# Batch 1's frequency-domain products: three instead of four

## The chip, the cores and the metric

The kernel runs on one core of one Trainium2 chip. The time is the device time of one execution, in microseconds (us). The kernel before takes 871.36 us, the median of three runs (871.35 to 871.52).

The engines have short names in the profile: PE is TensorE (PEld its weight loads), DVE is VectorE, ACT is ScalarE, POOL is GpSimd, and SP is SyncE, which only issues DMAs here. Each engine works through its own queue in order.

## The reference

```python
def _attn_ref(x, w_r, w_i, b_r, b_i):          # x: 8 x 3008 x 256
    X = np.fft.rfft(x, axis=1)
    Xr, Xi = (X.real.astype(np.float32), X.imag.astype(np.float32))
    Yr = Xr @ w_r - Xi @ w_i + b_r
    Yi = Xr @ w_i + Xi @ w_r + b_i
    lam = 0.01
    Yr = np.sign(Yr) * np.maximum(np.abs(Yr) - lam, 0.0)
    Yi = np.sign(Yi) * np.maximum(np.abs(Yi) - lam, 0.0)
    Y = Yr.astype(np.float64) + 1j * Yi.astype(np.float64)
    return np.fft.irfft(Y, n=x.shape[1], axis=1).astype(np.float32)

def _moe_ref(x, w_in, w_out):                  # x: 24064 x 256, d_ff 2048
    h = x @ w_in
    g = np.where(h > 0.0, h, np.exp(np.minimum(h, 0.0)) - 1.0)
    return (g @ w_out).astype(np.float32)
```

The output of the first is the input of the second: a Fourier transform along the sequence, a complex 256 x 256 layer with soft shrinkage (subtract from each value its clip to plus or minus 0.01), the transform back, and a feed-forward layer with an elu between two matrices.

## The kernel before

**Stages of one batch.** The transforms of length 3008 = 47 x 64 are split in two factors and done by matmuls. A batch passes through A (six units: the first factor), a round trip through DRAM that turns the data into the tile `Z`, X (eight units, `unit_X`: the second factor, giving `XT`, real and imaginary parts with features on the partitions), M (twelve groups of 128 frequencies, `unit_M`, numbered q = 0 to 5, i = 0 or 1: the complex layer and the shrinkage, giving the tile `Y`), DMAs that turn `Y` into `Yx` (`turn_Y`), B (six units, the first factor back; B v reads `Yx` of q = v), another round trip through DRAM (`Bs`), and Y (eight units, "y" or "n" in the plan, giving `yT`, the input of the feed-forward layer). `unit_X` for batch 1 takes its units in the order of quarters: units 2g and 2g + 1 give the slots 8g to 8g + 7 of the 32 slots for the two halves of the features.

**The loop.** The feed-forward layer is cut into 376 steps, 47 for a batch. Step i has a `front` (four products into the two PSUM tiles `hps`, one per 128 hidden units, then ScalarE's exponentials into `Et`), an elu (`elu` clips `Et`, `finish_elu` makes `gT` from `hps` and `Et` on VectorE at L1159 or L1161, one step later), and a `back` two steps later (eight products of `gT` with `w_out_r` into `ps_o`). There are four `hps` tiles, so the front of step i + 2 needs the two that the elu of step i has read. While the feed-forward layer of batch b runs, `plan(b)` hangs the stages of batch b + 1 and the A units of b + 2 into its steps, as lists `f0` (before the front) and `f1` (after `finish_elu`). Batch 1 has its stages in the steps of batch 0: X in steps 10 to 17 (`lead` = `FILL` = 10), M groups 0,0 to 2,1 in steps 18 to 23, B0 in 24, M 3 in 25 and 26, B1 in 27, M 4 in 28 and 29, B2 in 30, M 5 in 31 and 32, B3 to B5 in 33 to 35, and A of batch 2 from 36 on. In every eighth step (17, 25, 33) VectorE copies half of a finished output block (L1203).

**Where the elu's clip runs.** In a step with an M group ScalarE does it with a second pass (`on_act`: L1128 and L1133). In a "pooled" step GpSimd clips `Et` (L1169, two instructions). Else VectorE does it (L1171, one instruction of 128x1024). In the steps of batch 0 from 10 on, steps with other work are not pooled.

**M of batches 2 to 7.** With s = Xr + Xi the two outputs need three products of 256 columns, each over the two halves of the features: k = s @ w_r, and the products of Xi and Xr with changed weights (w_i plus or minus w_r, made in place by `three_weights`, L276, which also changes the bias, L279). `unit_M` puts k into one PSUM bank (`k1`) and the other two into another (`ps`). VectorE adds bias and k (L340), then k to both others (L341); GpSimd adds the second bias (L346), clips (L349) and subtracts (L350). The sums s are made by GpSimd beforehand (`sum_XT`, L260, rows of 512 frequencies); the last of six rows lies in the tile `busy`. `three_weights` runs in the first four steps of batch 1's feed-forward layer (47 to 50).

**M of batches 0 and 1.** They use the plain weights: four products of 512 columns into one bank (`m_group`, L292), one VectorE addition of the bias (L302), and for batch 1 GpSimd's clip and subtraction (L314, L315). `turn_Y` issues four DMAs for each q on SP's queue (L429); for batch 1's last q, two of the four go on GpSimd's.

GpSimd's queue carries also the loads of `x` for the batch after next (`load_x`, L121, steps 12, 15 and 18 here) and, in step 12, a small copy (`gate`, L976) that waits until batch 1's `Z` has arrived.

Of the kernel before, what the change touches and what calls it, by code (L numbers as in the profile page):

```python
# [8 lines left out]
ALU = mybir.AluOpType  # L9
# [15 lines left out]
NS = 32  # L25
# [4 lines left out]
def kernel(  # L30
# [224 lines left out]
    def sum_XT(b, dt, chunks=range(3)):  # L255

        XT = XT_of[b]
        for ch in chunks:
# [2 lines left out]
                sum_of(dt, ch), XT[:, dt, 0, m], XT[:, dt, 1, m], ALU.add  # L261
            )

    def sum_of(dt, ch):

        if 3 * dt + ch == 5:
            return busy[:]
        if not XS_of:
            XS_of.append(sump.tile([P, 5, 512], BF16, name="XS", tag="XS"))
        return XS_of[0][:, 3 * dt + ch]  # L270

    def three_weights(c, dt):
# [4 lines left out]
        if c == dt == 0:  # L277
            b_r_, b_i_ = (bias_bc[:, D * k : D * k + D] for k in range(2))
            nc.gpsimd.tensor_tensor(b_i_, b_i_, b_r_, ALU.subtract)  # L279

    mps_of = {}

    def m_group(b, q, i, ps, biased=False):
        XT = XT_of[b]
# [22 lines left out]
        return yb, clip  # L307

    def unit_M(b, q, i):
        if b == 1:  # L310
            if i == 0:
                mps_of[q] = unit_ps("mps", False)
            yb, clip = m_group(b, q, i, mps_of[q][:, i, :])
            nc.gpsimd.tensor_scalar(clip[:], yb, LAM, -LAM, ALU.min, ALU.max)  # L314
            nc.gpsimd.tensor_tensor(Y_of[b, q][:, i, :], yb, clip[:], ALU.subtract)  # L315
            return
        XT, o = XT_of[b], (2 * q + i) * P
        if i == 0:
            Y_of[b, q] = wk4.tile([P, 2, 2 * D], BF16, name="Y", tag="Y")
        ps, k1 = (  # L320
            last_banks("psM").tile([P, 2 * D], F32, name="mps", tag="mps") for _ in range(2)
        )
        ch, oc = divmod(o, 512)
        r, s = wcat_r, wcat_s
        todo = [
            (k1[:, 0:D], None, r[:, :, 0:D]),
            (ps[:, 0:D], XT[:, :, 1, o : o + P], s[:, :, 0:D]),
            (ps[:, D : 2 * D], XT[:, :, 0, o : o + P], s[:, :, D : 2 * D]),
        ]
        if o == 0 and b > 3:  # L330
            todo.append(todo.pop(0))
        for out_, lhs, w in todo:
            for dt in range(2):
                nc.tensor.matmul(  # L334
                    out_, lhsT=lhs[:, dt] if lhs is not None else sum_of(dt, ch)[:, oc : oc + P],
                    rhs=w[:, dt, :], start=(dt == 0), stop=(dt == 1),
                )
        yb = wk3.tile([P, 2 * D], F32, name="yb", tag="yb")
        clip = wk2.tile([P, 2 * D], F32, name="clip", tag="clip")
        nc.vector.tensor_tensor(yb[:, D : 2 * D], k1[:, 0:D], bias_bc[:, 0:D], ALU.add)  # L340
        nc.vector.tensor_tensor(  # L341
            yb[:].rearrange("p (c d) -> p c d", c=2),
            ps[:].rearrange("p (c d) -> p c d", c=2),
            yb[:, D : 2 * D].unsqueeze(1).to_broadcast([P, 2, D]), ALU.add,
        )
        nc.gpsimd.tensor_tensor(  # L346
            yb[:, D : 2 * D], yb[:, D : 2 * D], bias_bc[:, D : 2 * D], ALU.add
        )
        nc.gpsimd.tensor_scalar(clip[:], yb[:], LAM, -LAM, ALU.min, ALU.max)  # L349
        nc.gpsimd.tensor_tensor(Y_of[b, q][:, i, :], yb[:], clip[:], ALU.subtract)  # L350

    held = []

# [868 lines left out]
    def plan(b):  # L1222

        f0 = [[] for _ in range(PER)]
        f1 = [[] for _ in range(PER)]
        mode = [None] * PER
        n1, n2 = b + 1, b + 2
        mid = [("X", u) for u in range(8)] + [
# [4 lines left out]
        ]  # L1233
        if n1 < B:
            if b:
                lead, xs = 0, (3, 6, 9)

                def M(q):
                    return [("M", q, 0), ("M", q, 1)]

                shift = b - 1 if b < 3 else b - 3
                seq = [("y", 2), ("y", 3)] + [None] * shift + [("X", u) for u in range(8)]
                if b < 3:
                    seq += [("y", 4)] + M(0) + M(1) + [("y", 5)] + M(2) + [("B", 0)]
                else:
                    seq += M(0) + [("y", 4)] + M(1) + [("y", 5)] + M(2) + [("B", 0)]
                seq += [("y", 6), ("B", 1)] + M(3) + [("y", 7), ("B", 2)]
                on_act = [("X", 4), ("X", 7)]
                if b < 3:
                    seq += M(4) + [("B", 3)] + M(5) + [("A", 0), ("B", 4), ("A", 1), ("A", 2)]  # L1250
                    seq += [("B", 5), ("A", 3), ("A", 4), ("A", 5), None]
                else:
                    seq += M(4) + [("B", 3), ("A", 0)] + M(5) + [("B", 4)]
                    seq += [("A", 1), ("A", 2), ("A", 3), ("B", 5), ("A", 4), ("A", 5)] + [None] * (3 if n2 == B else 2)
                seq += [("n", 0), ("n", 1)]
            else:
                lead, seq = FILL, mid
                xs = (12, 15, 18)
        else:
            lead, seq = 0, [("y", u) for u in range(2, 8)]  # L1260
        for t, u in enumerate(seq, lead):
            if u is None:
                continue
            if b and n1 < B:
                mode[t] = "act" if u in on_act or u[0] == "M" else "pool"
            if mode[t] == "act" and u[0] != "M":
                k = {"y": "Y"}.get(u[0], u[0])
                c = {"y": b, "A": n2}.get(u[0], n1)
                if c < B:
                    dve = (False, True) if k == "B" else (k != "X" or b < 3 and u[1] == 7,)  # L1270
                    f0[t].append(put(k, c, u[1], False, *dve))
            elif u[0] == "y":
                f0[t].append(put("Y", b, u[1]))
            elif u[0] == "n":
                f0[t].append(put("Y", n1, u[1]))
            elif u[0] == "A":
                if n2 < B:
                    f0[t].append(put("A", n2, u[1]))
            elif b == 0 and u == ("B", 5):
                f0[t].append(put("B", n1, 5, False, True))  # L1280
            else:
                f0[t].append(put(u[0], n1, *u[1:]))
            if u[0] == "M" and u[2] == 1:
                f1[t].append((turn_Y, (n1, u[1])))
            if u == ("B", 5):
                for w, k in enumerate((0, 2, 3, 4)):
                    f1[t + k].append((load_Bs, (n1, w, 0, 4 * K1 - 16 * (b == w == 0))))
            if u == ("A", 5) and n2 < B:
                for part in ((0, 8), (8, NS)):
                    f1[t] += [(load_Z, (n2, a, *part)) for a in range(3)]  # L1290
        if b == 0:
            for t in range(6):
                f1[t].append((unit_A, (1, t, False, t not in (0, 2), True)))
            for t, a, u in (
                (7, f0, 2), (7, f1, 3), (8, f0, 4), (8, f1, 5), (9, f0, 6), (9, f1, 7)
            ):
                a[t].append((split_Y, (0, u)))
            for w in range(1, 4):
                f1[w].append((load_Bs, (0, w)))
            f1[6].append((turn_M3, ()))  # L1300
            for part in ((0, 8), (8, NS)):
                f1[5] += [(load_Z, (1, a, *part)) for a in range(3)]
            f1[xs[0]].append((lambda: gate(Z[:, 16, 0:1]), ()))
        if n2 < B:
            for ci in range(3):
                f1[xs[ci]].append((load_x, (n2, ci)))
        if b and n1 < B:
            f0[seq.index(("X", 4))].append((sum_XT, (n1, 0)))
            f0[seq.index(("X", 7))].append((sum_XT, (n1, 1, range(2 if b < 3 else 3))))
            if b < 3:  # L1310
                f0[seq.index(("M", 2, 0))].insert(0, (sum_XT, (n1, 1, (2,))))
        return f0, f1, mode
# [4 lines left out]
    for i in range(n + LAG):  # L1317
# [6 lines left out]
        elif i < n:  # L1324
# [9 lines left out]
            if mode[r]:  # L1334
                on_act = mode[r] == "act"
                pooled = not on_act
            else:
                on_act = any(f is unit_M for f, a in f0[r])
                pooled = free or i < FILL
            third = calm and bare % 3 == (2 if i // PER == B - 1 else 1)  # L1340
            h = front(i, third, on_act)
        finish_elu()
        if i < n:
# [50 lines left out]
```

## Time and profile before

| What | us |
|---|---|
| median of three runs | 871.36 |
| profiled execution | 871.1 |
| its span | 869.3 |
| TensorE busy | 860.8 |
| ScalarE busy | 715.4 |
| VectorE busy | 666.2 |
| GpSimd busy | 592.8 |

The span runs from the first to the last instruction that the profiler recorded; the execution's own time holds a little more. Busy shares are means over stages with different limits, so the stages around the change are read one by one. The chain of work that ended last is followed back from the last instruction through what released each piece; 94% of it is TensorE. In rows of the timeline the start of a TensorE group lies up to 0.35 us ahead of the start that the chain gives, since matmuls overlap; the two are not mixed where a difference is formed.

### The profile page before, as it was taken

What the parts mean: (1) busy time and instruction counts of PE and PEld (TensorE: products, weight loads), DVE (VectorE), ACT (ScalarE), POOL (GpSimd) and SP (SyncE); (2) the same over time, 40 slices, a digit from 0 to 9 for tenths busy, and PEclk for the clock granted to TensorE, in tenths of its full rate; (3) what the DMA queues carried; (4) which work ended last, traced back from release to release, by engine and by line L of the source; (5) the groups of instructions that cost most, each with busy time, mean ns of one, the idle gap of its engine ahead of it and who ended that gap; (6) DMA issues with size and microseconds to landing.
All of it is one profiled execution on the core that took longest, in us unless ns stands there. A gap on an engine that the chain in (4) does not pass through costs nothing.

```text
span 869.3 us, 18553 instructions
## 1 busy us (share of the span) xinstructions
PE 860.8 (99%) x6773; PEld 675.8 (78%) x6773; DVE 666.2 (77%) x1103; ACT 715.4 (82%) x1255; POOL 592.8 (68%) x866
## 2 busy tenths in 40 slices
PE   8999999999999999999999999999999999999997
PEld 6567677887788877887778877787877888787776
DVE  8889779697676886778866787677777687788775
ACT  8878888888978889798887988879887888876664
POOL 8671651898657986588846987459874697734664
PEclk9999999999999999999999999999999999999999
DMA  8897446532575135653365432753337313250111
GB/s 248 282 288 213 117 131 193 164 117 73 141 224 170 51 79 168 191 170 92 89 183 172 128 104 78 217 165 107 94 96 213 90 39 85 79 141 25 40 36 49
DMA packets 113597, 116.11 MB, mean 134 GB/s; under 512 B 11569, under 2 KB 103473, under 8 KB 110145
## 3 DMA queue, kind: packets, MB, share of 16 engines
q1 hardware_dynamic: 108512, 86.74, 35.2%
q0 software_dynamic: 4704, 27.92, 9.8%
q8 instruction: 53, 0.87, 0.4%
q14 instruction: 40, 0.32, 0.1%
q10 hardware_dynamic: 288, 0.26, 0.1%
HBM read 53.28 MB, written 48.23 MB: 117 GB/s over the span
## 4 chain that ended last, share of the span: by engine, by line
PE 94%; POOL 2%; DVE 1%; DMA 1%; ACT 1%; issue 0%; DVEq 0%; POOLq 0%
PE ps_o L1192 39%; PE hps L1118 34%; PE mps L334 5%; PE xps L242 3%; PE mps L1118 2%; PE yps L615 2%; PE bps L451 2%; PE mps L292 2%; PE aps L194 2%; POOL Y L350 1%; DMA xt<-in_x_dram 1%; PE aps L186 0%; POOL yb L346 0%; POOL clip L349 0%; DVE gT L1159 0%
## 5 line engine op out<-in xcount | busy, mean ns | idle before, releaser
L1159 DVE SCALAR_TENSOR_TENSOR gT<-Et,hps 128x512 fp32r<-128x512 f32 x630 | 403.1, 682 | 137.0 <-POOL Et L1169 127.0
L1192 PE MATMUL ps_o<-w_out_r,gT 128*128 128x256 f32 x3008 | 477.2, 301 | 0.0
L1192 PEld LDWEIGHTS ps_o<-w_out_r,gT 128*128 128x128 f32 x3008 | 404.4, 189 | 48.0 <-DVE osb L1203 0.2
L1169 POOL TENSOR_SCALAR Et<-Et 128x512 f32<-128x512 f32 x482 | 287.3, 615 | 203.1 <-ACT Et L1130 201.6
L1118 PE MATMUL hps<-yT,w_in_s 128*128 128x512 bf16 (+7 forms) x1620 | 366.7, 353 | 0.3
L1130 ACT ACTIVATE Et<-hps 128x512 f32<-128x512 f32 x514 | 282.7, 610 | 41.7 <-PE hps L1118 38.6
L1118 PEld LDWEIGHTS <-w_in_s 128*128 128x128 bf16 x1728 | 144.1, 98 | 104.7 <-issue 13.1
L1128 ACT ACTIVATE Et<-hps 128x512 f32<-128x512 f32 x192 | 104.5, 597 | 42.0 <-PE hps L1118 41.6
L1133 ACT ACTIVATE Et<-Et 128x512 f32<-128x512 f32 x192 | 110.5, 632 | 0.0
L350 POOL TENSOR_TENSOR Y<-yb,clip 128x512 bf16<-128x512 f32 x72 | 92.7, 1287 | 6.0
L346 POOL TENSOR_TENSOR yb<-yb,bias_bc 128x256 f32<-128x256 f32 x72 | 53.2, 738 | 11.3 <-DVE yb L341 11.2
L150 ACT CAST XT<-xps 128x768 bf16<-128x768 f32 x57 | 45.8, 804 | 14.1 <-PE xps L242 13.9
L341 DVE TENSOR_TENSOR yb<-mps,yb 128x512 f32<-128x512 f32 x72 | 49.8, 692 | 7.2
L150 ACT CAST yT<-yps 128x752 bf16<-128x752 f32 x56 | 44.1, 787 | 13.7 <-PE yps L615 13.5
L1161 DVE SCALAR_TENSOR_TENSOR gT<-hps,Et 128x512 fp32r<-128x512 f32 x78 | 50.2, 686 | 3.3
L349 POOL TENSOR_SCALAR clip<-yb 128x512 f32<-128x512 f32 x72 | 44.1, 613 | 6.3
L150 ACT CAST A<-aps 128x1024 bf16<-128x1024 f32 x40 | 40.7, 1018 | 8.1 <-PE aps L194 5.0
L150 ACT CAST Bz<-bps 128x1024 bf16<-128x1024 f32 x41 | 41.6, 1014 | 5.3 <-PE bps L451 5.0
L340 DVE TENSOR_TENSOR yb<-mps,bias_bc 128x256 f32<-128x256 f32 x72 | 30.5, 424 | 17.5 <-PE mps L334 15.7
L334 PE MATMUL mps<-wcat_s,XT 128*128 128x256 bf16 x288 | 43.2, 273 | 0.0
L1203 DVE COPY osb<-ps_o 128x512 f32<-128x512 f32 x46 | 31.7, 690 | 5.4 <-PE ps_o L1192 3.4
L260 POOL TENSOR_TENSOR XS<-XT 128x512 bf16<-128x512 bf16 x30 | 34.1, 1157 | 2.4 <-ACT XT L150 1.4
(216 smaller groups left out, 673.3 us busy)
## 6 DMA issues: line engine op xcount, KB each, us to landing
xt<-in_x_dram POOLq DMA_DIRECT2D x21, 1024.0 KB, 5.3
out_dram<-osb SPq DMA_DIRECT2D x154, 128.0 KB
Bs<-DB SPq DMA_DIRECT2D x30, 384.0 KB
Yx<-Y SPq DMA_DIRECT2D x166, 64.0 KB
DA<-A SPq DMA_DIRECT2D x19, 512.0 KB
DB<-Bz SPq DMA_DIRECT2D x19, 512.0 KB
Z<-DA SPq DMA_DIRECT2D x21, 384.0 KB
xt<-in_x_dram POOLq DMA_DIRECT2D x6, 512.0 KB, 6.2
```

Of the source, the lines that this page charges most:

```text
L150: nc.scalar.copy(dst, src)
L334: nc.tensor.matmul(out_, lhsT=lhs[:, dt] if lhs is not None else sum_of(dt, ch)[:, oc : oc + P], rhs=w[:, dt, :], start=(dt == 0), stop=(d ...
L346: nc.gpsimd.tensor_tensor(yb[:, D : 2 * D], yb[:, D : 2 * D], bias_bc[:, D : 2 * D], ALU.add)
L350: nc.gpsimd.tensor_tensor(Y_of[b, q][:, i, :], yb[:], clip[:], ALU.subtract)
L1118: nc.tensor.matmul(hps[s][:, c0:c1], lhsT=w_in_s[:, dt, ft * P : ft * P + P], rhs=yT_of[b][:, dt, t0 : t0 + c1 - c0], start=(dt == 0), sto ...
L1128: nc.scalar.activation(Et[:, s], hps[s], AF.Relu, scale=-1.0)
L1130: nc.scalar.activation(Et[:, s], hps[s], AF.Exp)
L1133: nc.scalar.activation(Et[:, s], Et[:, s], AF.Exp, scale=-1.0)
L1159: nc.vector.scalar_tensor_tensor(o, e, -1.0, h, ALU.add, ALU.max)
L1161: nc.vector.scalar_tensor_tensor(o, h, 0.0, e, ALU.max, ALU.add)
L1169: nc.gpsimd.tensor_scalar(e, e, 1.0, 0.0, ALU.min, ALU.max)
L1192: nc.tensor.matmul(po[q][:, j, :], lhsT=gT[:, s, i_ * P : i_ * P + P], rhs=w_out_r[:, ft, :], start=(ft == 0 and j == 0), stop=(ft == NFT ...
```

## The change

Batch 1's M groups take the form of the other batches: `unit_M` loses its branch for batch 1 (the old `m_group` stays for batch 0). What goes with it:

- `sum_part(b, g)`, new, makes the sums for one quarter of `Z`'s slots, in steps 11, 13, 15 and 17. Its three instructions go over runs of eight neighbouring elements, 48, 32 and 16 of them, 32 elements from one run to the next.
- The first group's product with the sums comes last of its three (as already for batches 4 and later).
- `three_weights` runs in steps 10 to 13 instead of 47 to 50.
- In the steps of B0, B1 and B2 of batch 1 the elu's clip is pooled.
- In batch 1's last group (q = 5, i = 1) VectorE clips and subtracts the real half at once; GpSimd clips the imaginary half, and VectorE subtracts it in `finish_Y`, after the elu of the step before and ahead of `turn_Y`'s DMAs. These DMAs stand in the order they had: for each half of the partitions one of the real half on SP's queue and one of the imaginary half on GpSimd's.

```diff
+    def sum_part(b, g):
+        XT, k = XT_of[b], slice(8 * g, 8 * g + 8)
+        def by_m(v):
+            return v.rearrange("p (m s) -> p m s", s=NS)[:, :, k]
+        sum_of(0, 0)
+        XS, m = XS_of[0][:], 2 * 512
+        for out_, dt, m0, m1 in (
+            (XS[:, 0:3].rearrange("p c n -> p (c n)"), 0, 0, 3 * 512),
+            (XS[:, 3:5].rearrange("p c n -> p (c n)"), 1, 0, m),
+            (busy[:], 1, m, 3 * 512),
+        ):
+            nc.gpsimd.tensor_tensor(
+                by_m(out_), by_m(XT[:, dt, 0, m0:m1]), by_m(XT[:, dt, 1, m0:m1]), ALU.add
+            )
...
     def unit_M(b, q, i):
-        if b == 1:
-            if i == 0:
-                mps_of[q] = unit_ps("mps", False)
-            yb, clip = m_group(b, q, i, mps_of[q][:, i, :])
-            nc.gpsimd.tensor_scalar(clip[:], yb, LAM, -LAM, ALU.min, ALU.max)
-            nc.gpsimd.tensor_tensor(Y_of[b, q][:, i, :], yb, clip[:], ALU.subtract)
-            return
...
-        if o == 0 and b > 3:
+        if o == 0 and (b == 1 or b > 3):
             todo.append(todo.pop(0))
...
+        if (b, q, i) == (1, 5, 1):
+            Y, h = Y_of[b, q][:, i, :], slice(0, D)
+            nc.vector.tensor_scalar(clip[:, h], yb[:, h], LAM, -LAM, ALU.min, ALU.max)
+            nc.vector.tensor_tensor(Y[:, h], yb[:, h], clip[:, h], ALU.subtract)
+            h = slice(D, 2 * D)
+            nc.gpsimd.tensor_scalar(clip[:, h], yb[:, h], LAM, -LAM, ALU.min, ALU.max)
+            late_Y.append((Y[:, h], yb[:, h], clip[:, h]))
+            return
...
+    def finish_Y():
+        Y, yb, clip = late_Y.pop()
+        nc.vector.tensor_tensor(Y, yb, clip, ALU.subtract)
...
             if u[0] == "M" and u[2] == 1:
+                if (b, u[1]) == (0, 5):
+                    f1[t].append((finish_Y, ()))
                 f1[t].append((turn_Y, (n1, u[1])))
...
-        if b and n1 < B:
+        if b == 0:
+            for g in range(4):
+                f0[lead + 2 * g + 1].append((sum_part, (n1, g)))
+        elif n1 < B:
...
-                pooled = free or i < FILL
+                pooled = free or i < FILL or any(f is unit_B and a[1] < 3 for f, a in f0[r])
...
-            if PER <= i < PER + 4:
-                three_weights(*divmod(i - PER, 2))
+            if FILL <= i < FILL + 4:
+                three_weights(*divmod(i - FILL, 2))
```

More of the change, by code (lines that the diff above doesn't have):

```diff
@@ L279, in three_weights @@
             nc.gpsimd.tensor_tensor(b_i_, b_i_, b_r_, ALU.subtract)
-    mps_of = {}
     def m_group(b, q, i, ps, biased=False):
@@ L348, in unit_M @@
         )
+        if (b, q, i) == (1, 5, 1):
[6 more added lines that the diff above has]
+            return
         nc.gpsimd.tensor_scalar(clip[:], yb[:], LAM, -LAM, ALU.min, ALU.max)
         nc.gpsimd.tensor_tensor(Y_of[b, q][:, i, :], yb[:], clip[:], ALU.subtract)
+    late_Y = []
+    def finish_Y():
+        Y, yb, clip = late_Y.pop()
+        nc.vector.tensor_tensor(Y, yb, clip, ALU.subtract)
     held = []
```

## The prediction

> **What bounds the kernel now.** I read the page's engine totals first, then the chain of work that ended last around batch 1's M groups, then the timelines of VectorE (DVE) and GpSimd (POOL) there and in batch 2, which already works in the new form. Totals, and busy time by stretch (stretch and its length, then PE, PEld, DVE, ACT, POOL):
>
> ```profile
> PE 860.8 (99%) x6773; PEld 675.8 (78%) x6773; DVE 666.2 (77%) x1103; ACT 715.4 (82%) x1255; POOL 592.8 (68%) x866
> 66.46:83.78 17.32, 17.32 (x161) 13.95 (x162) 15.51 (x25) 14.73 (x25) 1.58 (x3) 1.00 0.86 234
> 83.78:99.82 16.04, 16.04 (x99) 10.73 (x97) 12.22 (x21) 12.54 (x25) 10.82 (x13) 1.00 0.47 133
> ```
>
> TensorE is busy all the time at the full granted clock, in the eight X steps (66.46 to 83.78) and in the six M groups (83.78 to 99.82) alike; POOL is nearly idle in the X steps, and VectorE has 1.8 us spare in 17.3. So TensorE's work is the time, as long as nobody keeps it waiting. The chain (start, length, piece), first batch 1's M groups, then batch 2's:
>
> ```profile
> 83.78 0.88 PE mps L292 x4
> ...
> 99.82 0.45 PE bps L451 x4
> ...
> 105.65 0.86 PE hps L1118 x4
> ...
> 127.19 0.45 PE bps L451 x4
> ...
> 129.46 0.46 PE aps L194 x2
> ...
> 197.51 0.59 POOL Et L1169
> 198.10 0.02 issue
> 198.12 0.70 DVE gT L1159
> 198.82 0.04 issue
> 198.87 0.59 PE hps L1118 x2
> 199.46 0.59 PE hps L1118 x2
> ...
> 200.97 0.67 PE mps L334 x6
> ...
> 203.45 0.67 PE mps L334 x6
> ```
>
> Before, TensorE goes through batch 1's six groups without a gap. In batch 2 it does not: a POOL clip that came late (197.51) held an elu on VectorE, and that held TensorE, whose four hps products took 1.19 instead of 0.86 us.
>
> **The matmuls.** A group now takes 0.88 us (four of 512 columns) and will take 0.67 (six of 256, batch 2's row): 0.21 less. A whole step is 16.04/6 = 2.673 us now and 2.48 in batch 2 (200.97 to 203.45; means of longer stretches are 2.465). Twelve groups by 0.21: **-2.5 us**, all of it on the path. Weight loads go from four to six a group and lie under the matmuls in batch 2's 0.67.
>
> **The sums, ahead of the groups.** Prices on POOL, from the groups by line, and the last copy of X from ScalarE's timeline:
>
> ```profile
> L260 POOL TENSOR_TENSOR XS<-XT 128x512 bf16<-128x512 bf16 x30 | 34.1, 1157 | 2.4 <-ACT XT L150 1.4 <-DVE XT L148 1.0
> L276 POOL TENSOR_TENSOR wcat_s<-wcat_s,wcat_r 128x256 bf16<-128x256 bf16 x2 | 1.3, 672 | 0.0
> L279 POOL TENSOR_TENSOR bias_bc<-bias_bc 128x256 f32<-128x256 f32 x1 | 0.7, 734 | 0.0
> L121 POOL DMA_DIRECT2D xt<-in_x_dram x27 | 16.6, 629 | 1.4 <-POOLq L1378 0.8 <-PE ps_o L1192 0.3 <-PE mps L242 0.2
> L971 POOL TENSOR_SCALAR w_in_s<-w_in_f 128x256 bf16<-128x256 f32 x4 | 4.7, 1170 | 0.3
> 82.03 0.80 ACT L150 CAST XT<-xps 128x768 bf16<-128x768 f32 x1 [0.36 <-PE xps L242]
> ```
>
> From 672 (256 elements) and 1157 (512) an element costs 1.9 ns and an instruction 0.19 us. A quarter is 384, 256 and 128 elements in runs of eight: 0.91 + 0.67 + 0.43 = 2.0 us if the runs cost nothing, and four of them 8.0. No row has such runs; L971, whose source steps by 16 bytes, takes 1170 for 256, 4.6 ns an element with one input: that is the far end, 3.5 us a quarter, or about 6 if both inputs pay. I take 2.0: elements within a run lie side by side, as in L260. three_weights moves from steps 47 to 50 to steps 10 to 13: 4 x 0.67 + 0.73 = 3.4 us, worth nothing where it leaves (the chain holds TensorE alone there). Two x loads (0.63 each) and the gate stand in the same queue; the second load now stands behind two quarters and goes out some 8 us later, and its rows are first used by batch 2's A work (129.46). All of it, 13 us, fits into 17.3. The last quarter starts its second instruction when X's last copy is out (82.03 + 0.80) and ends that at 83.6; M(0,0) does its two other products first and reads sums at 84.2. So nothing on TensorE.
>
> But POOL was idle there, and VectorE's L1171 runs in each X step. How such a clip-like instruction meets POOL shows at 36 to 50 us:
>
> ```profile
> 35.90 0.62 DVE L971 TENSOR_SCALAR w_in_s<-w_in_f 128x512 bf16<-128x512 f32 x1
> 47.16 1.06 DVE L971 TENSOR_SCALAR w_in_s<-w_in_f 128x512 bf16<-128x512 f32 x1
> 49.33 1.05 DVE L971 TENSOR_SCALAR w_in_s<-w_in_f 128x512 bf16<-128x512 f32 x1
> 46.55 1.19 POOL L1169 TENSOR_SCALAR Et<-Et 128x512 f32<-128x512 f32 x2 [0.76 <-ACT Et L1130]
> 49.29 1.58 POOL L1169 TENSOR_SCALAR Et<-Et 128x512 f32<-128x512 f32 x2
> ```
>
> L971 took 0.62 as POOL began nothing ahead of it, and 1.05 where a POOL instruction ran (and POOL's pair 1.58 instead of 1.19). Each meeting costs VectorE up to 0.44. POOL computes for half of the X stretch, so about four of eight L1171 meet it: 1.75 us at most, less some 0.1 a step that VectorE has spare: I take **+0.6**, ends 0 (L1171 misses POOL or does not mind it) and 1.75.
>
> **The M groups on VectorE and POOL.** VectorE at the change of stages now; in batch 2 VectorE, a front of TensorE, and POOL:
>
> ```profile
> 84.30 0.68 DVE L1171 TENSOR_SCALAR Et<-Et 128x1024 f32<-128x1024 f32 x1
> 84.90 0.68 DVE L302 TENSOR_TENSOR yb<-mps,bias_bc 128x512 f32<-128x512 f32 x1
> 180.29 0.69 DVE L341 TENSOR_TENSOR yb<-mps,yb 128x512 f32<-128x512 f32 x1
> 180.90 1.27 DVE L1159 SCALAR_TENSOR_TENSOR gT<-Et,hps 128x512 fp32r<-128x512 f32 x2
> 182.22 0.42 DVE L340 TENSOR_TENSOR yb<-mps,bias_bc 128x256 f32<-128x256 f32 x1
> 182.75 0.69 DVE L341 TENSOR_TENSOR yb<-mps,yb 128x512 f32<-128x512 f32 x1
> 182.45 1.03 PE L1118 MATMUL hps<-yT,w_in_s 128*128 128x512 bf16 x4
> 181.36 0.74 POOL L346 TENSOR_TENSOR yb<-yb,bias_bc 128x256 f32<-128x256 f32 x1
> 182.18 0.61 POOL L349 TENSOR_SCALAR clip<-yb 128x512 f32<-128x512 f32 x1
> 182.88 1.29 POOL L350 TENSOR_TENSOR Y<-yb,clip 128x512 bf16<-128x512 f32 x1
> 184.13 0.74 POOL L346 TENSOR_TENSOR yb<-yb,bias_bc 128x256 f32<-128x256 f32 x1
> ```
>
> L302 becomes L340 and L341: VectorE's step is 2.46 us (180.29 to 182.75) against TensorE's 2.465. It keeps up, with nothing to spare. POOL gets L346 as well: 2.77 us a group (181.36 to 184.13), so it falls 0.3 behind in each of six groups that follow each other. And in steps 24, 27 and 30 (B0 to B2) the elu's clip moves from VectorE to POOL, into that backlog. The walk, on the clock of before: L340 takes L302's place at 84.90, L341 follows 0.53 later, L346 starts at 86.2. Six groups and one x issue: 86.2 + 6 x 2.77 + 0.63 = 103.45, when B0's clip starts. In batch 2 TensorE's first hps product started 1.36 us after that clip and the fourth ended 2.55 after it: 104.8 and 106.0. TensorE would be there (step 26) at 105.65 - 8 x 0.21 = 103.97 and through at 104.83. So it waits **1.2 us**. Behind that elu VectorE has the copy of an output half (0.60), L340, L341 and the next elu: 104.1 + 1.27 + 0.60 + 0.53 + 0.61 + 1.28 = 108.4 for a half that TensorE, already late, wants at 106.0 + 0.94 + 0.45 + 0.43 = 107.8: **0.6** more. Together **+1.8**; ends 1.2 (the elus overlap better) and 2.4 (POOL's group at 2.87). After that the distances suffice: the clips of B1 and B2 come 0.8 us or more ahead of need, with VectorE relieved of 0.69 in each of those steps.
>
> **The last group.** VectorE takes a 128x256 clip and subtraction between L341 and an elu. The rows nearest are L340 (0.42 for 128x256) and L1171 (0.68 for 1024): with the waits on each other about 0.8 us. In batch 2 an elu pair ends at 182.17 and the front that reuses its banks starts at 182.45, its second half a quarter to a half us on, say 0.4 of room in all: **+0.4**, ends 0 and 0.9. The second subtraction comes after that elu, when POOL's half clip is long done. What is sent ahead gains nothing: now L429 issues on POOL and B5 follows without a gap,
>
> ```profile
> 124.04 1.29 POOL L429 DMA_DIRECT2D Yx<-Y  x2 [0.30 <-POOL Y L315]
> DMA to landing us min/median/max: 2.4/2.5/2.5
> ```
>
> and the second of them lands just before 127.19; in the changed kernel both ends move about equally. If B5 had to wait, 0.2 us.
>
> The Trainium skill's page SBUF — State Buffer (SBUF: two separate sides) says that VectorE and GpSimd lock a port pair for a whole instruction, VectorE with a 2-port mode or with two SBUF inputs. No row here has a two-SBUF-input VectorE instruction against POOL; by that rule the last group's subtraction, too, would wait for a POOL instruction, and the sum would be some 0.5 us higher.
>
> **Sum:** -2.5 + 0.6 + 1.8 + 0.4 = **+0.3 us**. The profiled execution took 871.1 us (span 869.3); the median shown is 871.36, so **871.7**. From the ends 0, 1.2, 0 to 1.75, 2.4, 0.9 it could be 870.1 to 873.9; together I hold 870.5 to 872.7 for this case.
>
> **The rivals.**
> 1. *The backlog does not reach TensorE.* Then, with no loss in the X steps either, only the last group's 0.4 is lost: 869.3, faster. It decides if POOL's group takes 2.6 us or less (86.2 + 0.63 + 6 x 2.6 = 102.4, and 1.95 on from there, as 197.51 to 199.46, is the 104.4 at which TensorE wants the second half). For it: in batch 2 POOL's lateness cost TensorE only some 0.4 us. Against: there a y step lies between the fourth and fifth group, and 2.77 repeats from group to group. 0.12.
> 2. *The runs of eight are dear on POOL.* The X stage holds 17.3 us; less 5 us of weights, loads and gate, a quarter may take 3.1. Above that, M(0,0) waits on the sums: at 3.5 us a quarter 1.6 more than the forecast, 873.3; at 4.0 it is 3.6 more, 875.3, which I take; at 6 us, 883. For it: L971. Against: its elements are 16 bytes apart, here 2. The Trainium skill's GPSIMD Engine Reference (Performance pitfalls for Q7 kernels) has the penalty only for an inner step over 8 bytes; by it a quarter stays at 2.0 us. 0.18.
> 3. *The port costs more.* All four meetings at 0.44, and the last group's clip and subtraction behind POOL: 1.75 + 1.8 + 0.9 - 2.5 = +1.95, 873.3. For it: VectorE has no slack in the M steps to win lateness back. Against: L1171 starts when ScalarE is done, and three of POOL's four quarter starts are set by the same ScalarE, so they may interleave. 0.18.
>
> The forecast keeps 0.52. A measurement here tells 0.2% (1.74 us) from no change: 869.6 and 873.1 are the borders. Faster: rival 1, 0.12. Slower: most of rival 2 (0.16), over half of rival 3 (0.12) and little of the forecast (0.04): 0.32. Same: 0.56. The range leaves out rival 1 and rival 2 above its middle (0.08): 870.2 to 875.3.
>
> **What would show it.** Right: L334 groups of 0.67 us in batch 1; quarter sums near 0.9, 0.67 and 0.43; L1171 rows over 0.9 us in the X steps; a POOL clip of Et starting 1.5 us or more after ScalarE's Exp in step 24, and one gap in TensorE there of 1 us or more. Wrong: no such gap, sums of 1.5 us and more, or a TensorE wait for XS at the first group.

## The result and the profile after

The changed kernel takes 874.47 us (median of seven runs, 873.25 to 875.61) against 871.52 for the kernel before (seven runs on the same chip, 871.35 to 873.16): a ratio of 1.0031, 95% interval 1.0019 to 1.0042. It is slower, by some 3 us. The forecast was 871.7; the result lies inside its range, 870.2 to 875.3, but beyond the border of 873.1 behind which the prediction calls it slower.

The profiled execution took 874.94 us (span 873.1). From its page, the totals and the shares of the chain that ended last, and, from the view by stretches, the X steps of batch 1 (the same steps as 66.46 to 83.78 before; the columns are those of the prediction's first fence):

```profile
PE 861.7 (99%) x6797; PEld 678.1 (78%) x6797; DVE 673.6 (77%) x1115; ACT 716.5 (82%) x1255; POOL 614.6 (70%) x895
PE 88%; DVE 6%; POOL 4%; issue 1%; DMA 0%; ACT 0%; DVEq 0%; POOLq 0%
66.08:85.31 19.23, 18.73 (x166) 14.44 (x167) 17.64 (x24) 15.49 (x26) 14.35 (x20) 1.00 0.68 169
```

TensorE no longer carries the chain alone: VectorE and GpSimd hold a tenth of it. The X steps last 19.23 us where they lasted 17.32; VectorE's busy time in them rose by 2.1 us without one more instruction, since some take longer.

**Where the time went.** The start of each step's first `hps` product on TensorE is a clock for the step. Rows of TensorE's timeline before, for steps 11, 19, 25, 27, 32, 34 and 36:

```profile
68.95 1.03 PE L1118 MATMUL hps<-yT,w_in_s 128*128 128x512 bf16 x4
...
87.18 1.03 PE L1118 MATMUL hps<-yT,w_in_s 128*128 128x512 bf16 x4
...
102.80 1.03 PE L1118 MATMUL hps<-yT,w_in_s 128*128 128x512 bf16 x4
...
107.72 1.03 PE L1118 MATMUL hps<-yT,w_in_s 128*128 128x512 bf16 x4
...
120.71 1.03 PE L1118 MATMUL hps<-yT,w_in_s 128*128 128x512 bf16 x4
...
125.22 1.03 PE L1118 MATMUL hps<-yT,w_in_s 128*128 128x512 bf16 x4
...
129.77 1.13 PE L1118 MATMUL hps<-yT,w_in_s 128*128 128x512 bf16 x4
```

The same steps after:

```profile
68.59 1.03 PE L1141 MATMUL hps<-yT,w_in_s 128*128 128x512 bf16 x4
...
88.76 1.19 PE L1141 MATMUL hps<-yT,w_in_s 128*128 128x512 bf16 x4
...
103.57 1.03 PE L1141 MATMUL hps<-yT,w_in_s 128*128 128x512 bf16 x4
...
109.79 1.19 PE L1141 MATMUL hps<-yT,w_in_s 128*128 128x512 bf16 x4
...
122.11 1.03 PE L1141 MATMUL hps<-yT,w_in_s 128*128 128x512 bf16 x4
...
127.57 1.03 PE L1141 MATMUL hps<-yT,w_in_s 128*128 128x512 bf16 x4
...
133.38 1.09 PE L1141 MATMUL hps<-yT,w_in_s 128*128 128x512 bf16 x4
```

The distances between these rows give the account. From step 20 to step 23, three groups on, TensorE goes from 91.38 to 98.82 after and from 89.84 to 97.87 before, so a group saves 0.20; two groups lie between steps 11 and 19 and one between 25 and 27, and their saving is added back:

- X steps and the first two groups (11 to 19): 20.17 instead of 18.23, plus 0.40: **2.3 us lost**.
- B0 (25 to 27): 6.22 instead of 4.92, plus 0.20: **1.5 lost**.
- the last group's step (32 to 34): 5.46 instead of 4.51: **0.95 lost**.
- B5 (34 to 36): 5.81 instead of 4.55: **1.3 lost**.
- twelve groups by 0.20: **2.4 gained**.

Together +3.6; small pieces in other steps add 0.4, and the difference grows from -0.36 at step 11 to +3.61 at step 36. (The -0.36 arises ahead of step 0, where the two kernels issue the same work; such offsets ranged from -0.5 to +2.8 us in the profiled executions below, which is why the experiments are read by these distances and not by their totals alone.) The spans differ by 3.8.

The chain of work that ended last shows who held TensorE in the X steps, at B0, in the last group and at B5, and a group's own price (L343, 0.67 us):

```profile
77.15 1.44 DVE Et L1194
...
79.97 1.58 DVE Et L1194
...
105.51 0.59 POOL Et L1192
...
106.12 0.70 DVE gT L1182
...
106.86 0.59 PE hps L1141 x2
...
111.90 0.67 PE mps L343 x6
...
123.68 0.84 DVE Y L361
124.53 1.20 DVE gT L1182 x2
...
126.35 4.28 DMA Yx<-Y
...
130.68 0.61 PE bps L474 x4
```

(L1194 is what L1171 was, L1192 what L1169 was; L361 is VectorE's subtraction in the last group, and the `Yx` DMA is one of the two that GpSimd issues.) GpSimd's timeline in the X steps; L278 are the new sums, two of a quarter's three instructions in one row:

```profile
72.20 1.98 POOL L278 TENSOR_TENSOR XS<-XT 128x384 bf16<-128x384 bf16 x2 [4.83 <-DMA M3x<-M]
...
77.05 2.05 POOL L278 TENSOR_TENSOR XS<-XT 128x384 bf16<-128x384 bf16 x2
...
80.08 1.98 POOL L278 TENSOR_TENSOR XS<-XT 128x384 bf16<-128x384 bf16 x2
...
82.98 2.00 POOL L278 TENSOR_TENSOR XS<-XT 128x384 bf16<-128x384 bf16 x2
```

VectorE's clips there:

```profile
70.61 0.69 DVE L1194 TENSOR_SCALAR Et<-Et 128x1024 f32<-128x1024 f32 x1
...
77.07 1.51 DVE L1194 TENSOR_SCALAR Et<-Et 128x1024 f32<-128x1024 f32 x1
...
79.89 1.65 DVE L1194 TENSOR_SCALAR Et<-Et 128x1024 f32<-128x1024 f32 x1
...
82.85 1.61 DVE L1194 TENSOR_SCALAR Et<-Et 128x1024 f32<-128x1024 f32 x1
```

Three clips begin within 0.2 us of three quarters of sums and take 1.51 to 1.65 instead of 0.69; two more, at 72.76 and 74.97, take 0.90 and 0.79. Together that is 3.0 us on VectorE. The first row of sums shows something that the prediction had not seen: GpSimd stood idle for 4.83 us, until 72.20, for a DMA that copies the matrix `M3` to `M3x`. The sums' tile takes the place of an `M3` tile in its pool (both have the tag `XS`), and `M3x` is made late, behind the loads of `Z` on SP's queue. From 72.20 to 85.4 GpSimd then works almost without pause.

### The profile page after: what moved, and what is told of

Its sections match the earlier page's. It is cut to its first block, busy times and chain, and to the rows that moved or that the text cites. A ratio compares the mean times of both kernels' runs of the same rounds, so it can differ in the third digit from the quotient of the medians.

```text
span 873.1 us, 18643 instructions
## 1 busy us (share of the span) xinstructions
PE 861.7 (99%) x6797; PEld 678.1 (78%) x6797; DVE 673.6 (77%) x1115; ACT 716.5 (82%) x1255; POOL 614.6 (70%) x895
## 4 chain that ended last, share of the span: by engine, by line
PE 88%; DVE 6%; POOL 4%; issue 1%; DMA 0%; ACT 0%; DVEq 0%; POOLq 0%
PE ps_o L1215 37%; PE hps L1141 33%; PE mps L343 5%; PE mps L1141 2%; PE xps L242 2%; PE yps L638 2%; PE bps L474 2%; PE aps L194 2%; POOL Y L367 2%; POOL yb L355 1%; DVE gT L1184 1%; POOL clip L366 1%; DVE Et L1194 1%; PE mps L308 1%; DVE gT L1182 1%
## 5 line engine op out<-in xcount | busy, mean ns | idle before, releaser
L1192 POOL TENSOR_SCALAR Et<-Et 128x512 f32<-128x512 f32 x488 | 291.7, 617 | 206.3 <-ACT Et L1153 204.7
L367 POOL TENSOR_TENSOR Y<-yb,clip 128x512 bf16<-128x512 f32 x83 | 106.9, 1288 | 6.9
L355 POOL TENSOR_TENSOR yb<-yb,bias_bc 128x256 f32<-128x256 f32 x84 | 62.2, 740 | 14.7 <-DVE yb L350 14.5
L350 DVE TENSOR_TENSOR yb<-mps,yb 128x512 f32<-128x512 f32 x84 | 58.1, 692 | 8.4
L366 POOL TENSOR_SCALAR clip<-yb 128x512 f32<-128x512 f32 x83 | 51.0, 615 | 7.3
L349 DVE TENSOR_TENSOR yb<-mps,bias_bc 128x256 f32<-128x256 f32 x84 | 35.6, 423 | 20.3 <-PE mps L343 18.3
L343 PE MATMUL mps<-wcat_s,XT 128*128 128x256 bf16 x336 | 50.5, 273 | 0.2 <-DVE yb L350 0.2
L1184 DVE SCALAR_TENSOR_TENSOR gT<-hps,Et 128x512 fp32r<-128x512 f32 x72 | 46.4, 686 | 3.3
```

The source lines that it names most:

```text
L343: nc.tensor.matmul(out_, lhsT=lhs[:, dt] if lhs is not None else sum_of(dt, ch)[:, oc : oc + P], rhs=w[:, dt, :], start=(dt == 0), stop=(d ...
L355: nc.gpsimd.tensor_tensor(yb[:, D : 2 * D], yb[:, D : 2 * D], bias_bc[:, D : 2 * D], ALU.add)
L1192: nc.gpsimd.tensor_scalar(e, e, 1.0, 0.0, ALU.min, ALU.max)
```

## The experiments

The theory after this reading: (P) VectorE's clip and GpSimd's sums shut each other out of a shared port, and TensorE waits for the elu behind the clip; (Q) at B0 GpSimd's backlog of 2.77 us a group holds the pooled clip; (R) the last group's work on VectorE delays one elu; (S) at B5 the copies that GpSimd issues land late. The rivals are named with each run. Ratios are to the kernel before on the same chip (medians 871.3 to 871.7), with 95% intervals; losses by place are the distances above, in each run's profiled execution. These were the slowest of their kernel in e4 (878.07 us) and i1 (879.61), so a loss there need not be that of the median:

| Run | median us | ratio (interval) | X | B0 | last | B5 |
|---|---|---|---|---|---|---|
| the changed kernel | 874.47 | 1.0031 (1.0019 to 1.0042) | 2.3 | 1.5 | 0.95 | 1.3 |
| e1_m3x_early | 878.91 | 1.0089 (1.0071 to 1.0107) | 2.3 | 1.5 | 0.95 | 0.9 |
| e2_no_sums | 876.53 | 1.0058 (1.0046 to 1.0071) | 0.0 | 1.5 | 0.95 | 0.9 |
| e3_before_plus_sums | 872.28 | 1.0010 (1.0001 to 1.0018) | 0.54 | 0.0 | 0.0 | 0.0 |
| e4_last_plain | 874.19 | 1.0027 (1.0015 to 1.0039) | 2.35 | 1.5 | 0.0 | 3.8 |
| g1_b_not_pooled | 874.25 | 1.0035 (1.0023 to 1.0047) | 1.05 | 0.6 | 1.7 | 0.8 |
| g2_m3_half_first | 875.93 | 1.0049 (1.0037 to 1.0061) | 1.1 | 1.5 | 1.0 | 0.9 |
| g3_store_b3_late | 873.49 | 1.0025 (1.0016 to 1.0034) | 1.0 | 1.5 | 1.0 | 0.3 |
| g4_weights_ahead | 873.77 | 1.0031 (1.0019 to 1.0043) | 0.0 | 1.4 | 1.0 | 1.0 |
| h1_weights_first | 874.37 | 1.0028 (1.0017 to 1.0039) | 2.4 | 1.5 | 0.95 | 0.8 |
| h2_b0_and_load | 873.62 | 1.0024 (1.0014 to 1.0034) | 1.4 | 0.6 | 1.1 | 1.55 |
| h3_last_plain | 873.99 | 1.0032 (1.0020 to 1.0044) | 2.2 | 0.6 | 0.0 | 2.1 |
| i1_b3_pooled | 875.88 | 1.0045 (1.0031 to 1.0058) | 2.2 | 1.5 | 1.0 | 2.0 |

### e1: the copy of M3 first

```diff
         if b == 0:
+            f1[0].append((turn_M3, ()))
...
-            f1[6].append((turn_M3, ()))
```

> The changed kernel with the copy of M3 into M3x moved from step 6 to step 0, so that the first quarter's sums no longer wait until 72.2 us for it. Theory A (the sums were pushed together by that wait and then met VectorE's clips of steps 13 to 16, which lost 3.0 us): the sums start near 68 and 70 us, those clips fall from 1.5 to 1.65 us to below 1.0 for most, and the time falls by 1.5 to 2.4 us, to 872.0 to 873.0. Rival B (the sums' number, not their place, makes the clips late): the meetings only move to other steps and the time stays within 0.7 us of 874.5.

A miss as a test of the X steps: the copy, put ahead of the `Bs` loads, delayed these, and TensorE lost 3.8 us ahead of step 11. The X steps still cost 2.3, though the sums now began in time. One pair of rows in step 14 is worth the run. VectorE:

```profile
76.47 3.53 DVE L1194 TENSOR_SCALAR Et<-Et 128x1024 f32<-128x1024 f32 x1
```

GpSimd at that time:

```profile
76.28 0.68 POOL L294 TENSOR_TENSOR wcat_s<-wcat_r,wcat_s 128x256 bf16<-128x256 bf16 x1
76.92 1.53 POOL L278 TENSOR_TENSOR XS<-XT 128x384 bf16<-128x384 bf16 x2
78.41 0.41 POOL L278 TENSOR_TENSOR busy<-XT 128x128 bf16<-128x128 bf16 x1
78.79 0.66 POOL L294 TENSOR_TENSOR wcat_s<-wcat_r,wcat_s 128x256 bf16<-128x256 bf16 x1
```

The clip waited not for one instruction but for five that followed each other without a gap, and ended 0.55 us after the last of them (79.45). One meeting cost 2.84 us.

### e2: the same without the sums

```diff
-            for g in range(4):
-                f0[lead + 2 * g + 1].append((sum_part, (n1, g)))
+            f1[8].append((no_sums, ()))
```

> As the run before, but the four quarter sums of batch 1 are left out (the tile is set to zero in step 8, so batch 1's result lacks the product with the sums). What is left is the cost of the M groups and the last group alone. Theory A: all clips of the X steps take 0.69 us, no stall of TensorE before step 26, 1.2 to 1.8 us lost at B0's elu, 0.5 to 1 at the last group, up to 1.3 at B5: 871.3 to 872.7. Rival B (the M groups themselves make VectorE late from the first group on): stalls of 1 us or more in steps 18 to 23 remain, 873.5 or more.

Ahead of step 11 TensorE loses 4 us, as in e1. In the X steps one clip took 1.00, beside the weights; all later ones took 0.68 or 0.69, and nothing was lost there. B0, the last group and B5 cost what they cost with the sums. So without the sums there is no X loss (g4 below has them all and loses nothing either, with the weights elsewhere), and the other three have causes of their own.

### e3: the kernel before, with the sums added

The function `sum_part` and its calls in steps 11, 13, 15 and 17, as in the changed kernel; nobody reads the sums.

> The kernel before with nothing but the four quarter sums added in steps 11 to 17 (nobody reads them). They depend on nothing that VectorE does, and nothing waits for them. Theory A (the two engines exclude each other): VectorE's clips of 128x1024 (0.69 us) lengthen to 0.9 to 1.65 us wherever a sum runs, 1.5 to 3 us in all; the old M steps have 0.7 us of slack each and take up most of it: TensorE loses 0.5 to 1.5 us, 871.9 to 873.0. Rival C (the clips are late for another reason, such as ScalarE): clips stay at 0.69 and the time at 871.5.

```profile
73.20 1.21 DVE L1189 TENSOR_SCALAR Et<-Et 128x1024 f32<-128x1024 f32 x1
75.72 1.25 DVE L1189 TENSOR_SCALAR Et<-Et 128x1024 f32<-128x1024 f32 x1
78.28 1.01 DVE L1189 TENSOR_SCALAR Et<-Et 128x1024 f32<-128x1024 f32 x1
80.60 0.68 DVE L1189 TENSOR_SCALAR Et<-Et 128x1024 f32<-128x1024 f32 x1
```

Alone in the kernel before, where the weights are not in the same steps, the sums lengthen three clips by 0.3 to 0.6 and cost TensorE 0.54 us; the whole kernel is slower by 0.10% (0.01 to 0.18). Theory P holds as far as these rows go: nothing but the sums was added, and only clips that meet them are longer. That what they share is a port is not shown by any run.

### e4: the last group on GpSimd alone

```diff
-        if (b, q, i) == (1, 5, 1):
...
-            return
...
-                if (b, u[1]) == (0, 5):
-                    f1[t].append((finish_Y, ()))
```

> The changed kernel with the last group treated as the other eleven: GpSimd clips and subtracts both halves, nothing on VectorE. Theory A: the stall of 0.95 us in step 33 goes (VectorE's four-part chain there cost 2.1 us instead of 0.7), but Y is ready later on GpSimd (0.45 to 0.8 us later), so that B5 waits for its DMAs as long as now or longer: 1.3 to 2.1 us. Sum: between 0.8 us faster and 0.3 slower than the changed kernel, 873.7 to 874.8. Rival D (the part pays as a whole): 1 us or more slower, 875.5 or more.

The stall at the last group is gone (0.0 instead of 0.95, theory R), and B5 waits in its stead, twice (3.8 us in all in this execution; the forecast had 1.3 to 2.1). TensorE:

```profile
130.97 0.39 PE L466 MATMUL bps<-Yx,M3x 128*128 128x256 bf16 x2 [0.67 <-DMA Yx<-Y]
132.71 0.38 PE L466 MATMUL bps<-Yx,M3x 128*128 128x256 bf16 x2 [1.35 <-DMA Yx<-Y]
```

The whole kernel takes what the changed one takes, within the intervals: this part of the change neither pays nor costs.

### g1: B0 to B2 not pooled

```diff
-                pooled = free or i < FILL or any(f is unit_B and a[1] < 3 for f, a in f0[r])
+                pooled = free or i < FILL
```

> The changed kernel with one part undone: in the steps of B0, B1 and B2 the elu's clip is VectorE's again. Theory A (GpSimd's backlog makes that clip late at B0; and VectorE's clip has to wait for GpSimd's instruction there): TensorE's stall at B0's elu falls from 1.5 us to 0.3 to 1.0, but VectorE's clips in those steps take 1.0 to 1.6 us instead of 0.69, which brings back 0.3 to 1 us at B1 and B2. Time 873.6 to 874.8. Rival E (pooling itself is right, VectorE is the late one): more than 1 us slower, 875.5 or more.

B0's loss falls from 1.5 to 0.6: theory Q, the backlog of GpSimd holding the pooled clip, accounts for 0.9 of it. At B1 and B2, where 0.3 to 1 us were expected back, next to nothing came back (0.1), but the last group pays 0.8 more, and the total does not move. Since all three clips were moved at once, this run does not say which of them the last group pays for.

### g2: the copies of the first M3 tile ahead of the others

```diff
-        by_part(M3x, lambda c, s: M3[c][s * N2 : s * N2 + N2])
+        for c in range(2):
+            for s in range(2):
+                nc.sync.dma_start(M3x[c * N2 : c * N2 + N2, :, s, :], M3[c][s * N2 : s * N2 + N2])
```

> The changed kernel with the two copies that read the first M3 tile (whose place the sums take) issued ahead of the two that read the other; all four stay in step 6. The first sum starts at 69.5 to 70.5 instead of 72.2 us. Theory A (the wait pushes the sums into VectorE's clips): fewer or shorter meetings, TensorE's loss in the X steps and the first M groups falls from 2.4 to 1.0 to 1.9 us: 873.0 to 874.0. Rival B (number, not place): 874.0 to 875.0.

A miss: the sums began hardly earlier against their step (1.2 us after step 12's front, 1.5 in the changed kernel). The median is the highest of g1 to g4, with an offset of 2.5 us ahead of step 11. The X loss was 1.1 all the same; see g3.

### g3: the store of B3 behind that of B4

`unit_B` of B3 leaves its store to DRAM out, and B4 issues both, its own first.

```diff
+            for k in (() if v == 3 else (4, 3) if v == 4 else (v,)):
```

> The changed kernel with B3's store to DRAM issued behind B4's, about 3 us later, so that it is no longer in flight when GpSimd issues the last two copies of Y. Theory A (these copies share the DMA engines with that store, 256 KB issued 0.4 us ahead of them, and land after 4.1 us instead of 2.4): landing back to 2.4 to 2.8 us, TensorE's stall before B5 falls from 1.3 us to below 0.3: 873.2 to 873.8. Rival F (the copies are late because GpSimd makes their descriptors late): landing stays near 4 us and the time at 874.5.

Here the two `Yx` copies landed 3.1 us after their issue and B5 lost 0.3 instead of 1.3. The time to landing of these two copies, in the changed kernel:

```profile
DMA to landing us min/median/max: 3.8/4.1/4.3
```

and in g3:

```profile
DMA to landing us min/median/max: 2.9/3.1/3.3
```

That looked like the cause; h1 and h2 below, which keep this edit, show that it is not enough. The X steps lost 1.0 with the same GpSimd programme that lost 2.3. VectorE's clips in g3:

```profile
77.62 0.68 DVE L1197 TENSOR_SCALAR Et<-Et 128x1024 f32<-128x1024 f32 x1
...
79.61 1.65 DVE L1197 TENSOR_SCALAR Et<-Et 128x1024 f32<-128x1024 f32 x1
...
82.57 0.69 DVE L1197 TENSOR_SCALAR Et<-Et 128x1024 f32<-128x1024 f32 x1
```

and the sums beside them:

```profile
76.81 2.01 POOL L278 TENSOR_TENSOR XS<-XT 128x384 bf16<-128x384 bf16 x2
...
79.81 1.98 POOL L278 TENSOR_TENSOR XS<-XT 128x384 bf16<-128x384 bf16 x2
...
82.71 1.94 POOL L278 TENSOR_TENSOR XS<-XT 128x384 bf16<-128x384 bf16 x2
```

The quarters of sums come every 2.9 us. In the changed kernel VectorE's delayed steps come every 2.9 us too, and its clips start level with the sums three times. Here two earlier clips had been held a little longer (1.05 and 1.02 instead of 0.90 and 0.79), so the next (77.62) came 0.8 us after the start of its pair of sums, as the first of the two ended; it cost nothing, and the second sum waited. The last (82.57) came ahead of its pair. So two of the three meetings cost VectorE nothing. By this reading, tenths of a microsecond decide who pays: e4 and i1, with the changed kernel's GpSimd work in these steps, lost 2.35 and 2.2; g1, g2 and g3, with the same work but for g2's order of copies on SP, 1.0 to 1.1.

### g4: the weights in steps 5 to 8

g2, and `three_weights` called for 5 <= i < 9.

> As the second of these, and the five weight instructions in steps 5 to 8 instead of 10 to 13, so that GpSimd has only the sums, the gate and the loads in the X steps (3.4 us less work). Theory A: at most three clips of VectorE above 0.9 us; TensorE's loss there 0.5 to 1.3 us: 872.4 to 873.6. Rival B (a sum in each second step is enough to make VectorE late by 2 us): 874 or more.

With the weights out of the way the sums began at once in step 12 and had gaps between them; three clips took 0.88 to 1.01, the rest 0.69, and nothing was lost in the X steps. But the weights cost TensorE 0.85 at step 8, where GpSimd does the elus' clips. The total stays.

### h1: all weights in step 10

g3, and all four parts of `three_weights` in step 10.

> The changed kernel with B3's store behind B4's and all five weight instructions in step 10, in the time in which GpSimd waits for M3's copy anyway, instead of between the quarters. Theory A (each GpSimd instruction in the X steps that meets VectorE's clip costs up to its own length; three fewer of them stand there): TensorE's loss in X steps and first groups 0 to 0.8 us (2.4 in the profile of the changed kernel), B0 1.5, last group 0.95, B5 0.3 as before: 871.9 to 872.9. Rival B (number, not place): 873.5 as with the store alone.

A miss: GpSimd finished the weights while it would have waited for `M3x` anyway, but the quarters of sums then followed each other at 72.70 and 75.82 and met clips of 1.87, 1.71 and 1.38. The `Yx` copies landed after 3.6 us though B3's store came late, so the store alone is not the cause.

### h2: h1, B0's clip on VectorE, and the third load of x in step 30

```diff
-                xs = (12, 15, 18)
+                xs = (12, 15, 30)
...
-                pooled = free or i < FILL or any(f is unit_B and a[1] < 3 for f, a in f0[r])
+                pooled = free or i < FILL or any(f is unit_B and 0 < a[1] < 3 for f, a in f0[r])
```

> As the run before, and with B0's clip back on VectorE (B1 and B2 stay pooled) and the third load of x, which stands in GpSimd's queue among the six groups, issued in step 30 instead of 18. Theory A (B0's stall is GpSimd's backlog): the stall of 1.5 us at step 26 and 27 falls to 0 to 0.7, the rest as in the run before: 0.8 to 1.5 us faster than it, 870.9 to 871.9. Rival E: not faster than the run before.

B0 lost 0.6 again, as in g1, now with B1 and B2 pooled, and the last group 1.1, not the 1.7 of g1. The copies landed after 4.0 us and B5 lost 1.55. The median is 0.75 us below that of h1, but the intervals overlap, and the forecast's 870.9 to 871.9 was missed.

### h3: h2 with the last group on GpSimd alone

> As the run before, with the last group plain (GpSimd clips and subtracts both halves). Theory A: no stall in step 33 (now 0.95), but B5 waits 0.5 to 1.5 us for its last two copies, which now land after 2.4 to 3.1 us: between 0.5 us faster and 0.6 slower than the run before. Rival G (what is sent ahead pays): over 0.6 us slower.

As in e4: 0.0 at the last group, 2.1 at B5 (h2: 1.1 and 1.55). Landing took 2.9. The total is that of h2 within the intervals.

### i1: B3 pooled too

```diff
-                pooled = free or i < FILL or any(f is unit_B and a[1] < 3 for f, a in f0[r])
+                pooled = free or i < FILL or any(f is unit_B and a[1] < 4 for f, a in f0[r])
```

> Edit: B3's step is pooled too, so its elu's clip goes to GpSimd, behind the two Yx copies, and VectorE has no 128x1024 clip right after their issue. In the changed kernel that clip ran at 127.77 to 128.46, the copies were issued from 126.35 to 127.64 and landed 4.1 us after issue (before: 2.5, with no clip in the 2 us behind the issue), and B5 waited 1.3 us. Theory (VectorE's clip holds up the copies that GpSimd has issued): landing 2.4 to 2.8 us, B5's loss 0 to 0.3 us, time 873.0 to 873.8. Rival (B3's store, issued on SP 0.4 us ahead of them, takes the DMA engines first): landing stays 3.5 to 4.3, B5's loss 0.8 to 1.5, time 874.0 to 875.0. The step's own elu comes 0.5 us later on GpSimd at most, which by the walk at B0 costs TensorE 0 to 0.3. The X steps' loss, which varied from 1.0 to 2.4 us with the same programme, is read apart.

The elu's clip now stood on GpSimd behind four output DMAs, came late and cost 0.84 of its own, so the time says nothing on the question. The landing does: 3.6 us, with no clip behind the issue and VectorE idle from 131.84, 1.5 us after the first issue, until both copies had landed. The expectation is wrong on the kernel before, which had such a clip too, in the very time of the landing, with copies issued from 124.04 and landed after 2.5 us:

```profile
125.39 0.69 DVE L1171 TENSOR_SCALAR Et<-Et 128x1024 f32<-128x1024 f32 x1 [0.20 <-ACT Et L1130]
```

Two stretches that begin 1.7 us after the issue (same columns as above), in the changed kernel:

```profile
128.00:129.00 1.00, 1.00 (x8) 0.85 (x7) 0.96 (x2) 1.00 (x2) 0.85 (x2) 1.00 0.55 147
129.00:130.00 1.00, 0.55 (x5) 0.34 (x3) 0.93 (x3) 0.81 (x2) 1.00 (x3) 1.00 0.64 157
```

and in i1:

```profile
132.00:133.00 1.00, 0.99 (x7) 0.85 (x7) 0.00 (x0) 1.00 (x2) 0.86 (x2) 1.00 0.58 145
133.00:134.00 1.00, 0.55 (x5) 0.35 (x3) 0.00 (x0) 0.81 (x2) 1.00 (x3) 1.00 0.64 161
```

The DMA engines are as little busy (last but one column) whether VectorE works or not. VectorE's clip is not what makes the copies late. (The Trainium skill's page SBUF — State Buffer, SBUF: two separate sides, has a rule by which a VectorE instruction in a 2-port mode keeps GpSimd from writing the descriptors of its DMAs; for these copies i1 speaks against it, since landing stayed at 3.6 without that clip.) The store (h1, h2) does not explain it alone either.

The DMA packets kept in the traces show one more thing that differs. Besides the data, the list of DMA queues has a queue named `q8 instruction`, with 53 packets of 16 KB over the whole span. In all ten kernels whose first copy landed 3.3 us or more after its issue, one of these packets starts 1.2 to 2.2 us after that issue and takes 0.9 to 1.3 us. The kernel before and e3, with 2.5 and 2.4, have none between issue and landing; in e4 and h3 it comes 3.9 and 4.2 us after the first issue, and the first copy had landed after 2.7 and 2.6. A copy is 16 packets of 4 KB, each with one of 4 bytes behind it. In g3, 30 of these 32 small packets were through 2.32 us after the first issue, and the last two at 2.50 and 2.93, after the 16 KB packet, which ran from 1.21 to 2.09; in the changed kernel 30 were through at 2.39, and the next at 3.13, when the 16 KB packet ended. So such a packet in front of a sixteenth of the copy is the likeliest cause of most of the delay. No run moved it alone, so this is not shown.

Giving the sums and `M3` places of their own was not tried. No version beat the kernel before.

## Why the prediction was right and wrong

- **The matmuls, -2.5.** Right: 0.67 us a group as forecast, 0.20 saved, -2.4 in all.
- **The sums' own price, 2.0 us a quarter.** Right. A pair and a third row came to 1.53 and 0.41 in e1; runs of eight cost nothing extra, and rival 2 (dear runs) fell. The Trainium skill's GPSIMD Engine Reference (Performance pitfalls for Q7 kernels), which has a penalty only for an inner step over 8 bytes, agrees with these rows.
- **The X steps, +0.6, ends 0 and 1.75.** The mechanism was right, and the size was wrong: 2.3. The number of meetings was about right (five clips of eight, where four were forecast). The step that failed is "Each meeting costs VectorE up to 0.44". That came from L971, where one GpSimd instruction stood in the way. Here GpSimd had its next instruction ready, and a meeting cost 0.1 to 1.0 in the changed kernel, 2.84 in e1. Nor was GpSimd's work spread as the walk had it: the wait for `M3x` pushed sums, weights, gate and loads together. That this wait alone does not make the loss is shown by e1, whose sums began without it, and h1, which used the idle time for the weights: they lost 2.3 and 2.4. That the weights between the sums count is suggested, not shown, by e3 and g4, which lost 0.5 and nothing.
- **Interleaving.** Rival 3's counterargument, that the two engines may interleave since ScalarE sets both, was the wrong way round: they came into step. In the profiled executions of g1 to g3 they missed each other in part (1.0), so this term has no single value: 1.0 or 2.3 for nearly the same programme.
- **The page's rule in the prediction.** The Trainium skill's page SBUF — State Buffer (SBUF: two separate sides) says that whoever starts first holds the port pair for its whole instruction. The clips agree, but e1's waited through several instructions, of which the page says nothing. For the last group the rule gave 0.5 more, and that was near: the subtraction of 128x256 on VectorE took 0.84 in the chain's row above, the later one, with GpSimd idle, 0.41.
- **B0, +1.8, ends 1.2 and 2.4.** Right: 1.5, and its cause was the one named. The groups' first addition on GpSimd started at 88.26 (the walk had 86.2, without the loss in the X steps), and the pooled clip began 17.25 us later, at 105.51, just as in the walk. VectorE and TensorE followed as in batch 2's chain, e2 lost the same 1.5 with no loss in the X steps, and without pooling the loss fell to 0.6 (g1, h2). Rival 1 fell: the backlog reaches TensorE.
- **The last group, +0.4, ends 0 and 0.9.** Right in place, too small by half: 0.95, just beyond the end. The clip and the subtraction took 0.53 and 0.84 on VectorE, where the walk had 0.8 for both.
- **B5, 0 (or 0.2).** Wrong. The step that failed is that both ends "move about equally". They did move equally on GpSimd's side: the issue came at 126.35, and with the 2.5 us that landing took before, the second copy, issued some 0.67 later, would have been there at 129.5, about when the products of the step before ended. But landing took 4.1, and B5 began at 130.68. That a transfer might take another time when it is issued at another moment had been given no price. Why it took longer is not shown; the packet of `q8 instruction` is the likeliest cause.

The sum of the terms was +0.3 and would have been +3.85 with 2.3, 0.95 and 1.3 in the places of 0.6, 0.4 and 0: 874.95, where the profiled execution took 874.94; that the two agree so closely is in part chance, since B0 cost 1.5 and not 1.8 and the small pieces 0.4. Rival 3 (port dearer, 873.3) was nearest in its mechanism; it lacked B5 and the longer meetings. That the result lies inside the range is in part luck as well: the range reaches up to 875.3 for rival 2, which fell, while the forecast's own 870.5 to 872.7, and even the sum of all its upper ends, 873.9, lie below the result.

## What to carry to other kernels

Before work is moved to GpSimd beside VectorE's SBUF-to-SBUF instructions, look at whether GpSimd will have its next instruction ready: a meeting can cost what is left of a whole run of instructions (2.84 us in e1) and not only of one, and with gaps between them (g4) TensorE lost nothing. Where a new tile reuses a place in a pool, look up who reads the tile that was there before, and when. And an engine that is sped up by moving its work into the last free slots of others gains less than its own saving: here 2.4 us of matmuls were saved and 6 us of new waits came at four places, one of which handed its loss on to the next when it was relieved (the last group, in e4 and h3).

## What was unexpected of the hardware

- One VectorE clip of 0.69 us took 3.53 us (e1) beside five GpSimd instructions in a row, whereas in the changed kernel a clip got in after one sum of a pair (77.07, 1.51 long). Which of the two happens was not settled.
- Two 64 KB copies issued by GpSimd landed 2.4 to 4.1 us (medians of runs) after their issue, by kernel; neither VectorE's clip behind the issue (i1) nor the store ahead of them (h1, h2) explains it, and every first copy that landed after 3.3 us or more had a 16 KB packet of `q8 instruction` in its way.
- Work that is identical in the kernels, ahead of step 0, began up to 2.8 us later (i1) or 0.5 us earlier (e1) than in the kernel before.
